# A hand-written order of operations in attention plus GELU MLP: k and q of batch 2 loaded ahead of its v, DMA transposes by heads, w_out released by the fourth of them

## The chip, the cores and the metric

The kernel runs on one core of one Trainium2 chip. The metric is device microseconds of one execution; lower is better. Input and output lie in HBM in float32.

## What is computed

The reference is an attention without softmax (squared ReLU of the scaled scores, divided by the sequence length), followed by a two-layer MLP with exact GELU:

```python
# q, k, v: 8 batches x 12 heads x 448 x 64;  w_in: 768 x 2048;  w_out: 2048 x 768
scores = (1 / sqrt(64)) * q @ k^T
attn   = maximum(scores, 0) ** 2 / 448
x      = (attn @ v), heads side by side -> 3584 x 768
h      = x @ w_in
out    = (0.5 * h * (1 + erf(h / sqrt(2)))) @ w_out        # 3584 x 768
```

## The kernel before

**Work and tiles.** The work is cut by batch (b = 0 to 7) and, inside a batch, into three groups of four heads (g = 0 to 2). Everything is computed in bfloat16; GpSimd's DMA queue casts on the way in. For each batch the steps are:

- *loads*: k (`add_k`, line 546), q (`add_q`, lines 467 and 469) and v (`add_v`, line 567), each as one DMA per group, issued by GpSimd (POOL). w_in comes in five pieces (`add_win`), w_out in three (`add_wout`, line 490): piece 0 is the right half of the columns (one DMA of 1536 KB), pieces 1 and 2 are the left half (two DMAs of 384 KB each).
- *transposes*: batches 0 and 1 are transposed on TensorE (`add_tk`, `add_tq`, lines 608 and 635) with copies by DVE or ACT. From batch 2 on, `add_T_dma` does it with DMA transposes issued by SP (line 668); the code calls one of them a `turn`. A batch has nine turns: for each group one of k, one of the even and one of the odd columns of q. The odd one of group g also reads the first columns of group g + 1, so it waits for that load of q too.
- *QK* (`add_steps`, line 742): seven steps per group, four 64x64 matmuls of 448 columns each; ReLU on ACT or DVE (lines 754, 756), square on DVE (line 763).
- *AV* (`add_av`, line 805): 28 matmuls per group; two copies to xT by DVE or ACT (lines 511, 513).
- *F1* (`add_f1`, line 857): x @ w_in, 16 products of six matmuls per batch, GELU on ACT (line 867).
- *F2*: the first 256 rows as four plain products of 16 matmuls (`add_plain`, line 1270); (0, 1) and (1, 1) need only piece 0 of w_out, (0, 0) and (1, 0) all three. Later rows go in groups of 256 with seven products of half the depth in place of eight (`add_group`, line 1175). Those need sums of w_out's quadrants, which DVE builds (`add_tsums`, line 1111). From batch 5 on F1 is done in the same way (line 1001).

**What sets the order.** The program builds a list of operations, each with the operations that it depends on and the buffers that it takes and frees. The string `ORDER` at the top gives, word by word, which operation is next on which engine: P for TensorE (PE), A for ACT, D for DVE, G for GpSimd, S for SP, Z for a filler matmul; the number is the operation's place in the list. `Scheduler.place` walks through this string. Every engine executes its own words strictly in that order, so an operation that waits holds up all later ones on its engine. Waits come from the dependencies; the planner's costs have no influence on an operation that stands in `ORDER`.

**Buffers that matter here.** k and q before their transposition lie in one buffer each (`nk`, `nq`) from batch 2 on, so the loads of batch b + 1 wait until the turns of batch b have read them. kT and qT have two buffers, so the turns of batch b wait for QK of batch b - 2. PSUM has three double banks for QK and AV and two single banks for everything else.

**The gates.** GpSimd's queue is in order. A tiny copy on GpSimd that reads a transposed tile therefore holds back every load behind it until that turn has landed:

```python
def add_gate(b, g):
    def fn(e):
        n = (16 * g + 1) * KC
        nc.gpsimd.tensor_copy(gate, get_T(b)[0][:, n : n + 16 * KC : KC])

    deps = [Tq[b, g, c][0] for c in range(NC)] + [Tk[b, g, 0][0]]
```

It waits for all turns of q and k of the group. `add_gate(2, 0)` stands ahead of the first w_out load, `add_gate(2, 1)` ahead of piece 2, `add_gate(2, 2)` ahead of the loads of batch 3.

Of the kernel before, what the change touches and what calls it, by code (L numbers as in the profile page):

```python
# [18 lines left out]
NK = S // KB  # L19
# [62 lines left out]


ORDER = """
G1435 G0 A10 Z512 Z512 Z512 D13 Z512 G1 A16 Z512 P11 P17 G7 G3 D12 D18 P14 P42 G4 G121 D15 P21 D22
A43 P39 G2 P19 D44 A40 D20 P36 P29 P33 P48 G5 D41 A37 P31 P51 A49 D30 P23 P54 D32 G118 D34 A52 G6
P25 D24 P93 D26 P27 P63 G117 A55 P69 A94 P133 A64 D38 D28 A70 P57 Z512 G122 G9 D35 D56 P45 P90 D50
D134 A58 G8 Z512 P66 A91 D46 D71 G125 D47 A67 P131 D59 P81 Z512 D65 D68 P84 P108 A82 D53 D132 A85
P129 A109 P72 D92 A73 G126 P60 G120 D130 D86 A61 P96 G124 A74 P135 P102 G119 A62 P143 G128 D83
G123 A97 P78 A103 P105 D95 G127 P75 D136 D98 A144 A79 G147 P141 P111 D76 D104 A106 A142 D80 D77  # L90
G148 P99 P156 A112 P137 A100 G149 P171 D101 P139 A157 A172 D107 P168 P87 G150 D113 D110 G151 P114
S231 A169 D88 D138 A89 P159 A115 D140 A160 P195 A116 P145 P162 A146 D196 P219 D161 P204 A163 P251
D205 P243 D164 G152 G153 A220 P165 D170 A252 D158 A244 D173 P174 P180 A175 A181 D166 P259 P249
S229 P189 D176 A250 S232 D167 D190 P213 S228 A214 G154 P177 A178 P222 A260 P192 P265 P247 A266
D206 G155 A193 P267 D223 P207 D197 A179 S230 A248 D194 P183 P210 A268 P263 P253 D221 A208 D182
D211 P198 D224 A184 A264 A254 S234 D209 P216 P186 D191 G237 A187 P261 D199 D188 D212 D200 D185
A262 P255 P245 A217 P201 D215 D218 P225 G238 A256 P257 P288 D202 S233 S235 D226 A246 G239 A227
D203 D289 A258 P285 P294 A295 P372 P362 D286 S236 A373 P291 G240 D292 P276 P300 A363 P378 P356
A277 A379 D296 P376 A357 G241 P352 P303 G242 D301 P312 A377 P306 A353 P350 D313 P380 A351 D390
A381 P368 P370 G269 A369 P358 G270 A371 A359 P364 A365 D314 P354 P282 A355 D302 D304 D307 A283  # L100
D293 G271 G272 P279 P318 P366 G273 P348 A367 A349 P360 D305 D278 A361 D284 P374 G274 P382 A375
D319 D290 A280 D308 G275 D391 P330 P309 D287 D281 S398 P297 A331 D392 D320 S399 P315 P384 A298
D393 S401 A310 D396 A383 D417 P387 D394 A385 D419 A299 D311 A316 D395 P324 D317 P321 D418 A325
D397 P333 A388 P327 P421 D420 D322 S400 A328 P423 D323 A334 D326 S386 D422 P339 S402 P336 P342
D424 P425 D329 G407 G408 S403 A343 D335 P427 G409 A426 D337 S389 P429 A340 S404 D428 D344 P431
S405 D338 D341 P440 D332 P437 P345 D430 A438 D441 G410 P443 G411 P446 D432 P433 S406 A346 G412
D347 A444 P509 A447 D434 P511 D439 S435 D448 A510 S436 D442 P449 P452 P455 S541 D562 A512 P513
D445 A453 P515 D454 A450 A514 S542 P517 D456 G413 G414 D451 G415 P464 D457 S543 P461 P458 G416
A465 D462 A518 P467 P470 A516 P519 A459 P521 D471 A520 D472 P523 D466 A468 D460 A522 D560 P479
P476 P473 D469 A524 P525 D463 A477 P527 D480 A474 S544 D478 A526 P529 D475 A528 D481 P488 P485  # L110
P482 A489 D486 S545 A530 P494 P491 G550 P531 G551 D487 D483 G552 S546 P533 D495 A532 A484 P535
S547 D496 D561 A492 D490 A534 P503 P500 P497 D493 A536 P537 P564 D498 A538 D504 P539 A501 S548
D499 G553 A565 D505 G554 P600 D502 P603 G555 P506 S549 A601 D604 A540 P606 P609 P566 D563 A507
# [282 lines left out]
def kernel(  # L396
# [9 lines left out]
    nc = tc.nc  # L406
# [88 lines left out]
    def get_T(b):  # L495
        if b not in qkT:
            qkT[b] = (
                tpool.tile([128, SLOTS * KC], BF16, tag="qT", name="qT"),
                tpool.tile([128, G, NK * 128], BF16, tag="kT", name="kT"),
            )  # L500
        return qkT[b]
# [13 lines left out]
    def e_copy(n, psum=4):  # L515
# [4 lines left out]
    sch = Scheduler({"w": 3, "a": NA, "f": 2, "osb": 3, "s1": 1, "s2": 1, "s3": 1, "s4": 1,  # L520
                     "p": 1})
    pool_q, pe_q = [], []
# [8 lines left out]
    Tq, Tk = {}, {}  # L531
# [55 lines left out]
    def add_wout(i):  # L587
        c, rows = WOUTS[i]

        def fn():  # L590
            for kf in rows:
                load_wout(kf, c)

        n = ND * sum(kf.stop - kf.start for kf in rows)
        ld_wout[i] = dma(fn, n * 128 * 4, issues=len(rows))
# [64 lines left out]
    def add_T_dma(b, after):  # L660


        after = [list(x) for x in after]

        def turn(dst, src, deps):
            return sch.add(
                (("SP", T_STEP, T_TIME),),
                lambda e: nc.sync.dma_start_transpose(dst(), src()),  # L668
                deps + old_T(b) + after.pop(0), mode="X",
            )  # L670

        def slots_of(n, o, k):
            return lambda: get_T(b)[0].rearrange("p (s t) -> p s t", t=KC)[
                :, 2 * n + o : 2 * (n + k) + o - 1 : 2
            ]

        def q_src(n, o, k):
            return lambda: nq[b][:, 128 * n + D * o : 128 * (n + k) + D * o]

        def k_dst(g):  # L680
            return lambda: get_T(b)[1][:, g].rearrange("p (i t) -> p i t", t=128)

        def k_src(g):
            return lambda: nk[b][:, 2 * g : 2 * g + 2].rearrange("p e f -> p (e f)")

        n0, odd = 0, None
        for g in range(G):
            op = turn(k_dst(g), k_src(g), list(ld_k[b, g]))
            for i in range(NK):
                Tk[b, g, i] = (op, op)  # L690
            lands = list(dict.fromkeys(ld_q[b, g, c] for c in range(NC)))
            n = 8 * g + 9
            even = turn(slots_of(8 * g, 1, 8), q_src(8 * g, 1, 8), lands)
            prior = odd or even
            beyond = [ld_q[b, g + 1, c] for c in range(NC)] if g < G - 1 else []
            beyond = list(dict.fromkeys(beyond))
            odd = turn(slots_of(n0, 0, n - n0), q_src(n0, 0, n - n0), lands + beyond)
            n0 = n
            for c, o in enumerate((even, odd, prior, odd)):
                Tq[b, g, c] = (o, o)  # L700

    gate = const.tile([128, 16], BF16, tag="gate", name="gate")

    def add_gate(b, g):


        def fn(e):
            n = (16 * g + 1) * KC
            nc.gpsimd.tensor_copy(gate, get_T(b)[0][:, n : n + 16 * KC : KC])  # L709

        deps = [Tq[b, g, c][0] for c in range(NC)] + [Tk[b, g, 0][0]]
        pool_q.append(sch.add((("POOL", 0.2, 0.3),), fn, deps))

    xT, hT = {}, {}
    readers = {}
# [684 lines left out]
        add_load(2, g, g + 1)  # L1400
    add_steps(steps(1), ATT1_BIAS, True)
    add_T_dma(2, [[]] * 9)
    add_gate(2, 0)
    add_wout(0)
    add_wout(1)
    add_gate(2, 1)
    add_wout(2)
    add_gate(2, 2)
    for m in range(0, HALF_M, 2):
        add_f1(0, m, 1, bias=F1B_BIAS)  # L1410
# [135 lines left out]
```

## Time and profile before

| | |
|---|---|
| median of 3 runs | 378.59 us (377.18 to 379.72) |
| profiled execution | 377.22 us |
| its span | 375.4 us, granted TensorE clock 0.995 |
| TensorE busy | 360.1 us, 96% of the span |
| VectorE (DVE), ScalarE (ACT), GpSimd (POOL) busy | 285.4, 198.7, 64.7 us |
| chain that ended last | TensorE 83%, DMA 6%, ACT 4%, DVE 3% |
| DMA | 47.27 MB, mean 126 GB/s; 202 GB/s in the busiest early slices |

The profile is of one execution. A line of the timeline gives start and length in us, the engine, the line of the kernel, what was done and how often; in square brackets stands how long the engine had been idle before it and what released it. DMA lines give the issuing queue, the size and the time from issue to landing. PE is TensorE's matmul stream, SPq the DMA queue of SP, POOLq that of GpSimd.

### The profile page before, as it was taken

The numbers are of one execution on the slowest core, as the hardware profiler recorded it, in microseconds if no ns is written. First come the engines' busy times: TensorE is split into PE (matmuls) and PEld (weight loads), VectorE is DVE, ScalarE is ACT, GpSimd is POOL, SyncE is SP. The second block draws the span as 40 slices with busy tenths as digits, with TensorE's granted clock in tenths as the row PEclk, the third lists the DMA queues.
The fourth block names the chain that finished last, engine by engine and source line by source line (L and its number), as shares of the span: only waits on it lengthen the run. The fifth ranks groups of instructions, "written<-read, shape, count | busy, mean of one in ns | idle before, by whom it ended". The sixth has DMA issues, their size and how long they took to land.

```text
span 375.4 us, 8364 instructions
## 1 busy us (share of the span) xinstructions
PE 360.1 (96%) x3517; PEld 219.3 (58%) x3517; DVE 285.4 (76%) x473; ACT 198.7 (53%) x319; POOL 64.7 (17%) x103
## 2 busy tenths in 40 slices
PE   7989998599999999999999999999999999999995
PEld 3666554245554445554455544456985897688663
DVE  2989875168888898989498996998868558755872
ACT  3988755145555663856876567764540263045200
POOL 8575404320231233012220000000000000000000
PEclk9999999899999999999999999999999999999999
DMA  9999999999999999999996980002002300310222
GB/s 169 202 201 205 202 181 167 182 201 178 156 200 196 160 204 159 202 188 184 182 158 103 201 166 3 0 2 84 2 2 84 86 3 15 99 57 0 86 84 84
DMA packets 87812, 47.27 MB, mean 126 GB/s; under 512 B 53856, under 2 KB 84320, under 8 KB 87776
## 3 DMA queue, kind: packets, MB, share of 16 engines
q0 software_dynamic: 31376, 22.45, 41.8%
q1 hardware_dynamic: 55760, 23.79, 32.7%
q8 instruction: 27, 0.44, 0.5%
q10 hardware_dynamic: 640, 0.51, 0.4%
q14 instruction: 9, 0.07, 0.1%
HBM read 45.61 MB, written 11.01 MB: 151 GB/s over the span
## 4 chain that ended last, share of the span: by engine, by line
PE 83%; DMA 6%; ACT 4%; DVE 3%; SPq 1%; issue 1%; POOL 0%; DVEq 0%; ACTq 0%; POOLq 0%
PE pso L1175 31%; PE psh L857 20%; PE pb L1001 13%; PE ps L742 8%; PE pav L805 7%; DMA wout_sb<-in_moe_w_out_dram 4%; ACT a_sq L754 4%; PE pso L1270 3%; DMA nq<-in_q_dram 2%; SPq L668 1%; DMA qT<-nq 1%; DVE a_sq L763 1%; DVE part L1038 1%; DVE a_sq L756 1%; PE tp L635 0%
## 5 line engine op out<-in xcount | busy, mean ns | idle before, releaser
L754 ACT ACTIVATE a_sq<-ps 128x896 bf16<-128x896 f32 (+1 forms) x120 | 105.0, 918 | 39.7 <-PE ps L742 39.5
L763 DVE TENSOR_TENSOR a_sq<-a_sq 128x896 bf16<-128x896 bf16 (+1 forms) x169 | 97.2, 616 | 14.0 <-ACT a_sq L754 13.6
L857 PE MATMUL psh<-xT,win_sb 128*128 128x448 bf16 (+1 forms) x516 | 96.6, 340 | 0.0
L857 PEld LDWEIGHTS <-win_sb 128*128 128x128 bf16 x516 | 48.0, 98 | 45.6 <-issue 9.7
L756 DVE TENSOR_SCALAR a_sq<-ps 128x896 bf16<-128x896 f32 x49 | 53.0, 1087 | 14.0 <-PE ps L742 13.9
L867 ACT ACTIVATE h_sb<-psh 128x448 bf16<-128x448 f32 x80 | 43.3, 549 | 27.6 <-PE psh L857 27.3
L1175 PEld LDWEIGHTS <-s_sb 128*128 128x128 bf16 x424 | 40.7, 98 | 26.7 <-issue 2.1
L1038 DVE TENSOR_TENSOR part<-pb,part 128x448 f32<-128x448 f32 x60 | 34.6, 620 | 21.5 <-PE pb L1001 21.5
L742 PE MATMUL ps<-qT,kT 64*64 64x448 bf16 (+1 forms) x756 | 48.0, 336 | 2.0 <-DMA qT<-nq 1.7
L1175 PEld LDWEIGHTS <-h_sb 128*128 128x128 bf16 x312 | 29.6, 98 | 21.9 <-issue 3.8
L805 PE MATMUL pav<-a_sq,v_sb 64*64 64x448 bf16 (+1 forms) x756 | 36.7, 329 | 1.7 <-issue 1.5
L1175 PE MATMUL pso<-wout_sb,s_sb 128*128 128x384 bf16 (+2 forms) x216 | 38.1, 320 | 0.1
L1175 PE MATMUL pso<-wout_sb,h_sb 128*128 128x384 bf16 x208 | 38.1, 326 | 0.0
L1175 PE MATMUL pso<-t_sb,s_sb 128*128 128x384 bf16 x208 | 38.1, 326 | 0.0
L742 PEld LDWEIGHTS <-kT 64*64 64x64 bf16 x756 | 18.3, 105 | 23.2 <-issue 17.4
L1047 ACT ACTIVATE h_sb<-part 128x448 bf16<-128x448 f32 x36 | 20.1, 578 | 20.2 <-DVE part L1038 19.9
L805 PEld LDWEIGHTS <-v_sb 64*64 64x64 bf16 x756 | 21.4, 107 | 13.4 <-issue 2.8
L1209 DVE TENSOR_TENSOR osb<-pso,p_sb 128x384 f32<-128x384 f32 x39 | 21.6, 554 | 10.0 <-PE pso L1175 7.4
L1001 PEld LDWEIGHTS <-win_sb 128*128 128x128 bf16 x288 | 27.6, 98 | 2.3 <-issue 0.4
L709 POOL COPY gate<-qT 128x16 bf16<-128x16 bf16 x15 | 5.7, 380 | 109.6 <-DMA qT<-nq 109.6
L1001 PEld LDWEIGHTS <-ws 128*128 128x128 bf16 x216 | 20.7, 98 | 0.0
L513 ACT CAST xT<-pav 128x448 bf16<-128x448 f32 (+1 forms) x33 | 16.0, 494 | 8.8 <-PE pav L805 5.6
(60 smaller groups left out, 295.4 us busy)
## 6 DMA issues: line engine op xcount, KB each, us to landing
nk<-in_k_dram POOLq DMA_DIRECT2D x23, 224.0 KB, 6.0
nq<-in_q_dram POOLq DMA_DIRECT2D x21, 224.0 KB, 6.8
out_dram<-osb SPq DMA_DIRECT2D x20, 192.0 KB, 3.8
v_sb<-in_v_dram POOLq DMA_DIRECT2D x5, 672.0 KB, 11.0
v_sb<-in_v_dram POOLq DMA_DIRECT2D x9, 224.0 KB, 9.0
out_dram<-osb SPq DMA_DIRECT2D x6, 336.0 KB, 2.9
win_sb<-in_moe_w_in_dram POOLq DMA_DIRECT2D x8, 192.0 KB, 9.1
wout_sb<-in_moe_w_out_dram POOLq DMA_DIRECT2D x1, 1536.0 KB, 14.4
```

Of the source, the lines that this page charges most:

```text
L742: nc.tensor.matmul(ps[64 * j : 64 * j + 64, e, x * w : x * w + w], kT[r, g, i * 128 + 64 * j : i * 128 + 64 * j + 64], moving, start=True, ...
L754: A.activation(ar, ps, AF.Relu, scale=c_att)
L756: V.tensor_scalar(ar, ps, c_att, 0.0, op0=mybir.AluOpType.mult, op1=mybir.AluOpType.max,)
L763: V.tensor_mul(box["a2"][:, :, :used], ar, ar)
L805: nc.tensor.matmul(pav[0][o2 : o2 + 64, e, :w], vt[b][r, 2 * g + e, bass.ts(i, D)], box["a2"][r, y, o : o + w], start=(i == 0), stop=(i == ...
L857: nc.tensor.matmul(ph[:, x * n : x * n + n], win_sb[:, kd, bass.ts(m + x, 128)], xT[b][:, kd, c], start=(kd == 0), stop=(kd == KD - 1),)
L867: A.activation(h_ring()[:, m : m + nm, o + c.start : o + c.stop], box[0][:, :S].rearrange("p (x n) -> p x n", x=nm), AF.Gelu,)
L1001: nc.tensor.matmul(bank[name][:, y, z * HS : z * HS + HS], w[:, k, bass.ts(mm, 128)], right()[:, k], start=first and k == 0 and z == 0, st ...
L1038: V.tensor_add(get(to), ps(name), get(other))
L1047: A.activation(h_ring()[:, m : m + 2, o + half[c].start : o + half[c].stop], src().rearrange("p (x n) -> p x n", x=2), AF.Gelu,)
L1175: nc.tensor.matmul(box[bank][:, n0:n1], left()[:, kf], right()[:, kf, n0:n1], start=bool(need) and kf == 0, stop=kf == K2 - 1, skip_group_ ...
L1209: V.tensor_add(out()[:, n0:n1], box[bank][:, n0:n1], other()[:, n0:n1])
```

## The change

One line of the program's list is exchanged, one small function is added for it, and `ORDER` is new up to about the ninth F1 product of batch 2:

```diff
+    def add_kgate(b, g):
+
+        def fn(e):
+            nc.gpsimd.tensor_copy(gate, get_T(b)[1][:, g, :: NK * 8])
+
+        pool_q.append(sch.add((("POOL", 0.2, 0.3),), fn, [Tk[b, g, 0][0]]))
...
     add_T_dma(2, [[]] * 9)
-    add_gate(2, 0)
+    add_kgate(2, 1)
     add_wout(0)
```

`add_kgate(2, 1)` waits for one turn alone, that of k of group 1. Lines behind it in the file move by six (709 becomes 708 for the old gate, 1270 becomes 1276, and so on).

`ORDER` has 26 changed lines of 79; a few of them:

```diff
-G1435 G0 A10 Z512 Z512 Z512 D13 Z512 G1 A16 Z512 P11 P17 G7 G3 D12 D18 P14 P42 G4 G121 D15 P21 D22
+D13 G0 A10 Z512 G1 Z512 G7 G1435 P11 P14 A16 D12 P17 D15 A18 P33 P19 P21 D20 A34 A22 P39 G3 P42
...
-A262 P255 P245 A217 P201 D215 D218 P225 G238 A256 P257 P288 D202 S233 S235 D226 A246 G239 A227
+P263 G238 D194 D191 P201 A264 D221 A256 S234 A202 P225 D226 P288 A203 P282 D227 P257 D289 A258
...
```

Read by queue, that is:

```
SP, turns of batch 2 (group: k, q even, q odd)
  before: k1 qe0 qe1 k0 qo0 k2 qo1 qe2 qo2
  after:  k0 qe0 qo0 k1 qe1 qo1 k2 qe2 qo2

GpSimd, from the loads of batch 2
  before: k0 q0 v0 k1 q1 v1 k2 q2 v2 gate(2,0) w_out0 w_out1 gate(2,1) w_out2 gate(2,2) loads of batch 3
  after:  k0 q0 v0 k1 q1 k2 q2 kgate(2,1) w_out0 v1 w_out1 v2 w_out2 gate(2,1) gate(2,2) loads of batch 3
  and the identity matrix (line 1330) made after the first three loads, not ahead of them

TensorE, from the last AV of batch 1 to the first QK of batch 3 (the number of operations)
  before: F1, 3 QK, 2 F1, 3 QK, 4 F1, 3 QK, F1, plain(0,1), 5 F1, 3 QK, 4 F1, plain(1,1), 2 QK, AV,
          QK, plain(0,0), plain(1,0), QK, AV, 2 QK, 2 products, 3 QK, 4 products, QK of batch 3
  after:  2 QK, F1, 3 F1, 3 QK, 4 F1, 3 QK, 2 F1, 3 QK, 3 F1, plain(0,1), 2 F1, 2 QK, AV,
          2 QK, 2 F1, plain(0,0), plain(1,1), 3 QK, product, plain(1,0), QK, QK of batch 3, AV, ...
```

The first F1 named is the last one of batch 0 in both, the others are of batch 1. Ahead of that AV the same operations stand on TensorE in another order, with two of the eight filler matmuls at the start and six further on (before: five and three). A few copies and ReLUs change between ACT and DVE (DVE 470 operations before and 469 after, ACT 317 and 318). No matmul, load or store is added or taken away.

More of the change, by code (lines that the diff above doesn't have):

```diff
@@ L84 @@
 ORDER = """
-G1435 G0 A10 Z512 Z512 Z512 D13 Z512 G1 A16 Z512 P11 P17 G7 G3 D12 D18 P14 P42 G4 G121 D15 P21 D22
[L86 to L95, printed above, removed]
@@ L96 @@
-D211 P198 D224 A184 A264 A254 S234 D209 P216 P186 D191 G237 A187 P261 D199 D188 D212 D200 D185
-A262 P255 P245 A217 P201 D215 D218 P225 G238 A256 P257 P288 D202 S233 S235 D226 A246 G239 A227
[L98 to L107, printed above, removed]
@@ L108 @@
-D445 A453 P515 D454 A450 A514 S542 P517 D456 G413 G414 D451 G415 P464 D457 S543 P461 P458 G416
-A465 D462 A518 P467 P470 A516 P519 A459 P521 D471 A520 D472 P523 D466 A468 D460 A522 D560 P479
-P476 P473 D469 A524 P525 D463 A477 P527 D480 A474 S544 D478 A526 P529 D475 A528 D481 P488 P485
+D13 G0 A10 Z512 G1 Z512 G7 G1435 P11 P14 A16 D12 P17 D15 A18 P33 P19 P21 D20 A34 A22 P39 G3 P42
+A43 Z512 P48 D40 D44 G4 P29 P36 D35 D30 P23 A49 P54 D24 A37 P51 G121 P25 D26 Z512 A52 A55 D41 P63
+P66 A67 P27 P90 D64 D50 G2 P31 P69 D28 G5 D32 A91 P57 Z512 D38 D53 Z512 Z512 G118 A58 D59 D65 P102
@@ new lines @@
+A103 D68 P93 A70 G6 P133 A94 P45 D46 D56 G117 G122 D134 P84 A47 G9 P129 P108 G8 D95 P60 A85 D61
+A109 P131 A62 P96 D71 P75 A97 D130 D132 P72 D73 Z512 P78 A76 P135 A74 A79 G125 P156 P143 G126 A157
+D86 P105 P111 G120 G124 D98 D136 A144 P165 A166 D92 D110 D77 D112 A106 D104 P141 D113 P81 P99 G119
+G128 D107 P139 D100 A82 D80 P162 A142 A101 P114 P174 D83 G123 D115 G127 A163 P137 G147 D116 A175
+P87 G148 A88 P159 D140 G149 P168 D138 A169 D89 D176 P145 S228 P243 G150 P210 A146 P183 D160 D167
+A244 P216 D161 P251 A184 A252 D217 P189 A211 P171 G151 S229 S230 D158 D170 S231 D185 P249 A172
@@ new lines @@
+P259 D164 D173 P198 A190 P180 A250 P177 A181 D199 P219 A260 G153 P186 P253 D212 D182 D218 S232
+A178 A220 D179 P247 D187 D200 A254 P207 P222 P195 A248 D223 P265 A208 D209 P261 A196 G154 A266
+D188 P204 S233 P192 P213 P245 D205 D224 A262 A214 D206 A246 D215 A193 G237 P267 D197 P255 A268
+P263 G238 D194 D191 P201 A264 D221 A256 S234 A202 P225 D226 P288 A203 P282 D227 P257 D289 A258
+P374 D283 P348 A375 P354 D290 P291 A349 D292 P300 P276 P366 D277 A355 G152 A367 D293 P364 A365
+A301 P358 P370 A359 P285 G239 P294 P279 S235 P350 D286 A371 A280 P372 G155 S236 P303 A295 P306
@@ new lines @@
+P312 A351 A373 G241 P356 P376 D281 G240 A357 P360 G242 A307 A377 G269 A361 P380 G270 D313 D308
+D302 D287 A381 D278 D284 A304 P362 D390 D314 P352 P342 D391 S398 D296 S399 A353 P318 D343 D344
+A319 P297 A298 P309 D392 G271 G272 P333 A363 D393 D394 D320 S401 P368 A369 P378 A379 D417 D299
+P384 D395 P382 A385 P330 A310 A334 P327 S400 P315 D418 G273 P421 A316 A328 D311 D305 A422 D383
+P387 A331 D397 P336 D317 P443 D396 P321 D419 D329 S386 D335 A337 P324 A388 P423 D322 P425 A444
+A325 D326 A323 D420 G274 D424 A426 P437 P449 D338 P339 D340 S402 G275 G407 D332 P427 G408 P429
@@ L111 @@
+P455 S403 A438 D428 A450 D341 G409 A456 D430 P440 D441 P345 P470 D560 P467 D562 D471 P431 D445
+A346 A347 D432 P433 A468 P446 D434 A447 D451 P452 P461 P513 A514 D453 P523 P521 D439 G410 A524
+P517 A522 G411 P515 G412 A518 A516 P511 D457 P509 D448 D454 D462 S389 S404 A512 D442 S405 A510
+P464 S406 A465 S435 P476 S436 P458 P479 S541 D477 G413 P473 G414 P519 P525 D472 G415 G416 A459
+A460 D466 D469 A520 S542 S543 D463 P527 D480 A474 S544 D478 A526 P529 D475 A528 D481 P488 P485
 P482 A489 D486 S545 A530 P494 P491 G550 P531 G551 D487 D483 G552 S546 P533 D495 A532 A484 P535
```

## The prediction

> **What bounds the kernel now.** I read the page first: the shares, the slices, the chain that ended last; then the PE timeline around its idle stretches, the waits of the queues, and windows of 2 us with the DMA columns.
>
> ```profile
> span 375.4 us, 8364 instructions
> PE 360.1 (96%) x3517; PEld 219.3 (58%) x3517; DVE 285.4 (76%) x473; ACT 198.7 (53%) x319; POOL 64.7 (17%) x103
> ...
> PE   7989998599999999999999999999999999999995
> ...
> DMA  9999999999999999999996980002002300310222
> ```
>
> TensorE is busy for 96% of the span, so only its 15 us without work and its slow stretches can be won. The slices (9.4 us each) put the losses into the first slices and into the eighth (the 5, 66 to 75 us). The DMA engines stand at 9 up to slice 22: in this part every transfer queues behind others. The PE timeline shows the two idle stretches and their releasers (start, length, engine, line, count, idle before):
>
> ```profile
> 54.82 1.31 PE L857 MATMUL psh<-xT,win_sb 128*128 128x448 bf16 x6
> 57.81 0.76 PE L742 MATMUL ps<-qT,kT 64*64 64x448 bf16 x12 [1.68 <-DMA qT<-nq]
> ...
> 66.91 1.31 PE L857 MATMUL psh<-xT,win_sb 128*128 128x448 bf16 x6
> 72.68 4.21 PE L1270 MATMUL pso<-wout_sb,h_sb 128*128 128x384 bf16 x16 [4.46 <-DMA wout_sb<-in_moe_w_out_dram]
> ...
> 87.73 2.76 PE L1270 MATMUL pso<-wout_sb,h_sb 128*128 128x384 bf16 x16
> ```
>
> The first QK of batch 2 waits 1.68 us for a turn (a DMA transpose) of q, the first plain product 4.46 us for w_out. That product then takes 4.21 us; the same sixteen matmuls take 2.76 at 87.73. The windows say why: the clock stood at 0.55 and 0.59.
>
> ```profile
> 68.00:70.00 2.00, 0.21 (x2) 0.00 (x0) 0.00 (x0) 0.54 (x1) 0.00 (x0) 1.00 1.27 192
> 70.00:72.00 2.00, 0.00 (x0) 0.00 (x0) 0.00 (x0) 0.00 (x0) 0.21 (x1) 1.00 1.32 199
> 72.00:74.00 2.00, 1.32 (x5) 0.65 (x6) 0.00 (x0) 0.00 (x0) 1.65 (x3) 0.55 1.32 203
> 74.00:76.00 2.00, 2.00 (x9) 1.02 (x8) 1.26 (x2) 0.00 (x0) 1.89 (x3) 0.59 1.31 205
> ```
>
> (Columns: window, length, busy PE, PEld, DVE, ACT, POOL, clock, DMA share, GB/s.) All engines stand still while the DMA engines run full. The chain names what holds them:
>
> ```profile
> 54.27 3.40 DMA qT<-nq
> 57.81 0.21 POOL gate L709
> 58.02 0.24 issue
> 58.26 14.37 DMA wout_sb<-in_moe_w_out_dram
> 72.68 4.21 PE pso L1270 x16
> ```
>
> The fifth turn lands at 57.7, the gate copy on GpSimd follows, w_out is issued at 58.26 and its first part lands 14.4 us later. From 76.7 to 248 us PE never idles, so whatever reaches PE in the front goes through to the end, as long as nothing later comes due too early.
>
> **The change, part by part.** From about the ninth product of F1 of batch 2 (PE at 124.96 us) on, the instructions of every engine stand in the same order in both kernels. So the question is when PE reaches that point.
>
> *k and q ahead of v, turns by heads.* In before, the copies of batch 2 land one behind another, about 1.15 us apart: k of group 0 at 43.0 (issue 34.21 + 8.8), k of group 1 at 46.4, the last q at 51.6 (42.32 + 9.3), the last v at 52.7 (43.26 + 9.4). SP's first turn wants k of group 1, so it starts at 46.51. In the changed kernel it wants k of group 0: SP starts at 43.0. A turn alone lands 3.2 to 3.4 us after its issue, and SP issues one every 1.3 us; but beside queued copies it crawls:
>
> ```profile
> kT<-nk SPq DMA_TRANSPOSE x1, 3.2
> ...
> qT<-nq SPq DMA_TRANSPOSE x1, 7.2
> ...
> qT<-nq SPq DMA_TRANSPOSE x1, 11.6
> ...
> kT<-nk SPq DMA_TRANSPOSE x1, 9.3
> ```
>
> (Four single issues, us to landing: at 52.9 with the copies drained, at 58.4 and 59.8 beside w_out, at 81.6 beside k and q of batch 3.) So the early turns gain little until the copies drain. One v fewer stands before the last q (1.3 us), and the identity matrix moved behind three DMA issues on GpSimd starts all loads some 0.3 us sooner: the copies drain at about 50.1 instead of 52.7. In before the first three turns land 0.7, 1.5 and 2.3 us after the drain; the same gives 50.8, 51.6 and 52.4, and group 0 is complete. QK of batch 2 is wanted at 54.7 (below): the 1.68 us go.
>
> *w_out after the fourth turn.* The fourth (k of group 1) is issued when SP is free, at 50.4, and lands 3.2 us later, 53.6. Landing to w_out's issue took 0.6 us (57.67 to 58.26): issue at 54.2, 4.0 us earlier. With 14.4 us its first part lands at 68.6. Bounds: 12.5 us (1.57 MB at the 203 GB/s of the full windows, plus the 4 to 5 us that a copy of 224 KB takes when the queue is short) and 18.1 us (the longest w_out issue): 66.7 to 72.3. In the single software queue two v copies (1.15 us each) now stand among the w_out parts, so its last part lands at 80.4 - 4.0 + 2.3 = 78.7.
>
> [...]
>
> *The new order on PE.* Ahead of the first plain product stand five more F1 (6 matmuls, 1.14 us each) and two more QK (0.2 us): 6.1 us of cover moved forward from behind it. From the end of the last AV of batch 1 (54.7): 13 F1 = 14.8 us and 11 QK in four bunches (0.50 for two, 0.69 for three from the chain's x8 and x12) = 2.6: PE arrives at 72.2 without idling. w_out is there at 68.6 (72.3 by the upper bound). So the 4.46 us go, and with them the slow clock, 4.04 us to the next product instead of 2.6: 1.45. Together 1.68 + 4.46 + 1.45 = 7.6 us. If the cover were gone, 4.46 would come back less the 4.0.
>
> *What is late next.* PE then runs on to the first QK of batch 3, which the new order places before the second AV of batch 2. From 72.2: four plain (10.4), four F1 (4.6), eight QK (2.2 with the changes of tile form), one AV (1.3), one product of group 1 (1.3): 92.0; the first QK of batch 3 stood at 108.5 before. It needs the last turn of group 0 of batch 3, which landed at 90.11 + 5.8 = 95.9. k and q of batch 3 queue behind w_out, whose end moves by 1.7 us: 94.2. With PE 0.3 us earlier (next part), 91.7, it waits 2.5 us; behind it in PE's queue stand the AV and all that follows, and DVE's copies of that AV wait as well. Bounds: 0 (the turns land early) and 5.5 (one more turn beside copies, 3.2 us more). The gates of groups 1 and 2 now follow the last w_out issue on GpSimd; they release k of batch 3 only when the last q turn lands, 71.3 before, some 72.5 now, and copies still queue until 78.7, which hides this.
>
> *The front up to 53 us.* PE's work there is the same. DVE and ACT are busy without a gap from 10 to 20 us, so order shifts little; the first q of group 1 lands 0.3 us sooner where PE waits 1.03 us. I take 0.3 us gained, between 1.5 lost and 2.0 gained (its own gaps sum to 3.2). The DVE sees one operation fewer (469 against 470) and is at most 95% busy in 90 to 100 us; no price.
>
> *Sum:* 7.6 + 0.3 - 2.5 = 5.4 gained; I take off 0.2 for DVE running late after the new stall: 5.2. The profiled execution took 377.22 us (span 375.4): 372.0. It lies 1.4 under the median of the runs shown (378.59; 377.18 to 379.72), so as a median **373.4 us**. About 1% is what a measurement of this kernel tells from no change.
>
> **The rivals.** (1) *The new stall does not come:* turns of batch 3 land by 92. For it: the DMA windows 50 to 52 (99 GB/s) and 58 to 62 (155, 127) hold some 2 us of unused transfer that earlier turns and w_out could fill. Then 7.6 - 0.2: 371.2. (2) *The stall grows and the clock falls with it:* a wait of 4 to 5 us and 1.5 us of half clock as after 72.7. Gain 7.9 - 4.5 - 1.5 = 1.9: 376.7. For it: the turns beside copies took 7 to 11 us. [...] (3) *Slower:* the third turn beside w_out starves until the copies end. Then the last q turn of batch 2 lands at 79 instead of 72.5, gate and k of batch 3 follow at 79.8, k lands 5.5 us later (as 96.61 to 102.1) at 85.3, and the last turn of group 0, 14.4 us behind it as in before, at 99.7. PE waits 7.6 us plus 1.5 of clock, 9.1 against 7.9 won: 379.8; it is a loss from 98.5 us on, and 383 if k of group 1 starves too. Against it: the two turns beside w_out landed 5.7 us apart, so a third lands by 73 if it starts 4 us sooner. (4) *The early release does nothing* since bytes rule: w_out lands at 72.6 as before. The new order still hides it, but batch 3 comes at 98: as (2) or (3).
>
> **How the numbers follow.** Forecast 0.55 (371 to 375.5), (1) 0.13, (2) with (4) 0.20, (3) 0.12. Faster by over 1% means under 374.8: 0.49 of the forecast and all of (1), 0.62; slower needs 382.4, the far half of (3) and accidents of the new front, 0.12; the rest 0.26. The range 370.2 to 379.6 reaches from (1) to (3).
>
> **What would show it.** Right: QK of batch 2 starts at 54 to 55 with no idle; w_out issued near 54, its first part landed by 70; the plain product at full clock; one PE idle of about 2 us on a turn of q at 92 to 95. Wrong: the gate copy after 56, a plain product still waiting, idle above 4 us at the first QK of batch 3, or new PE gaps before 50 us.

## The result and the profile after

The changed kernel takes 376.08 us (374.81 to 378.09) against 378.03 us (375.26 to 379.72) for the kernel before: a ratio of 0.9959, 95% interval 0.9940 to 0.9977. That is a gain of 1.6 us (0.9 to 2.3), where 5.2 had been forecast; 376.08 is near the 376.7 of rival (2). The two profiled executions lie closer together than the medians (376.74 against 377.22, spans 375.0 and 375.4; the one 0.7 above its median, the other 0.8 below), so what follows accounts for the 0.5 us between them; the rest of the gain is not in this pair. The granted clock may hold a part of it: of 29 executions of the kernel before that were measured beside the later experiments, 26 had a mean clock of 0.988 to 0.993 and only three the 0.995 of the profiled one, while 13 of the changed kernel's 17 had the 0.990 or 0.991 of its profile. So the profiled execution of the kernel before lost less to the half clock than most.

The page of the changed kernel, its span, shares and slices:

```profile
span 375.0 us, 8360 instructions
PE 361.1 (96%) x3517; PEld 219.8 (59%) x3517; DVE 284.2 (76%) x472; ACT 200.5 (53%) x320; POOL 63.5 (17%) x103
...
PE   8999999997599999999999999999999999999995
...
DMA  9999999999999999999998970002002300310222
```

TensorE's weak slices have moved: the eighth (66 to 75 us) is full now, the tenth and eleventh (84 to 103 us) are the 7 and the 5. The PE timeline says by what (start, length, engine, line, count, idle before and its releaser):

```profile
54.02 0.55 PE L748 MATMUL ps<-qT,kT 64*64 64x448 bf16 x8
...
68.25 3.58 PE L863 MATMUL psh<-xT,win_sb 128*128 128x448 bf16 x18
71.66 2.76 PE L1276 MATMUL pso<-wout_sb,h_sb 128*128 128x384 bf16 x16
...
91.46 0.38 PE L748 MATMUL ps<-qT,kT 64*64 64x448 bf16 x4
97.61 0.59 PE L748 MATMUL ps<-qT,kT 64*64 64x448 bf16 x4 [5.77 <-DMA qT<-nq]
```

Both old stalls are gone: QK of batch 2 starts at 54.02 with no idle before it, the first plain product at 71.66, at once and at full clock (2.76 us, not 4.21). In their place stands one stall of 5.77 us at the first QK of batch 3. The windows of 2 us around it show its second price:

```profile
92.00:94.00 2.00, 0.00 (x0) 0.00 (x0) 0.00 (x0) 1.18 (x2) 0.00 (x0) 1.00 1.35 158
94.00:96.00 2.00, 0.00 (x0) 0.00 (x0) 0.00 (x0) 0.00 (x0) 0.00 (x0) 0.73 1.28 147
96.00:98.00 2.00, 0.39 (x8) 0.26 (x12) 0.00 (x0) 0.00 (x0) 0.21 (x1) 0.50 1.15 227
98.00:100.00 2.00, 2.00 (x28) 1.20 (x24) 0.00 (x0) 0.92 (x1) 1.43 (x2) 0.50 1.22 225
100.00:102.00 2.00, 2.00 (x20) 0.74 (x12) 0.62 (x1) 0.77 (x1) 0.00 (x0) 0.57 1.12 70
```

(Columns as before: the last three are granted clock, DMA share, GB/s.) The clock falls at 94.9 and comes back at 101.7, 6.8 us at half speed. The AV at 97.95 takes 2.61 us to the next start instead of 1.32, and with the operations around it that is 2.0 us lost after the stall itself. The chain of waits names the way there:

```profile
49.67 4.71 DMA kT<-nk
54.38 0.05 issue
54.44 0.20 POOL gate L716
...
92.61 4.87 DMA qT<-nq
97.47 0.14 issue
97.61 0.59 PE ps L748 x4
```

The fourth turn lands at 54.38 and w_out is issued at 54.67, 3.6 us sooner than before. But the last part of w_out lands at 82.38, where it was 80.39 before (two v copies now stand among its parts, 2.3 us by the prediction's 1.15 us each), and the turn that QK of batch 3 wants lands at 97.47, where it was 95.92.

The balance of the two profiles at the ninth F1 product of batch 2, from which the orders agree: 7.59 us of old stalls and slow clock gone, 0.7 won in the front (the last AV of batch 1 starts at 52.70, before 53.39), 5.77 and 2.0 lost. That is 0.5 us, and the product starts at 124.51 instead of 124.96.

### The profile page after: what moved, and what is told of

The parts are those of the page before. It is cut to its first block, busy times and chain, and to the rows that moved or that the text cites. A ratio compares the mean times of both kernels' runs of the same rounds, so it can differ in the third digit from the quotient of the medians.

```text
span 375.0 us, 8360 instructions
## 1 busy us (share of the span) xinstructions
PE 361.1 (96%) x3517; PEld 219.8 (59%) x3517; DVE 284.2 (76%) x472; ACT 200.5 (53%) x320; POOL 63.5 (17%) x103
## 4 chain that ended last, share of the span: by engine, by line
PE 73%; DMA 18%; SPq 3%; DVE 2%; issue 1%; POOL 1%; ACT 0%; DVEq 0%; POOLq 0%; ACTq 0%
PE pso L1181 31%; PE psh L863 16%; PE pb L1007 13%; PE ps L748 7%; DMA nq<-in_q_dram 6%; PE pav L811 6%; DMA wout_sb<-in_moe_w_out_dram 4%; SPq L668 3%; DMA win_sb<-in_moe_w_in_dram 3%; DMA nk<-in_k_dram 2%; DMA qT<-nq 1%; DMA kT<-nk 1%; DVE a_sq L769 1%; PE pso L1276 1%; DVE part L1044 1%
## 5 line engine op out<-in xcount | busy, mean ns | idle before, releaser
L760 ACT ACTIVATE a_sq<-ps 128x896 bf16<-128x896 f32 x120 | 105.7, 918 | 38.4 <-PE ps L748 37.9
L762 DVE TENSOR_SCALAR a_sq<-ps 128x896 bf16<-128x896 f32 (+1 forms) x49 | 52.5, 1077 | 16.4 <-PE ps L748 16.2
L811 PE MATMUL pav<-a_sq,v_sb 64*64 64x448 bf16 (+1 forms) x756 | 38.0, 338 | 1.0 <-issue 0.8
L511 DVE CAST xT<-pav 128x448 bf16<-128x448 f32 (+1 forms) x22 | 11.7, 545 | 14.0 <-PE pav L811 13.8
L708 POOL COPY gate<-qT 128x16 bf16<-128x16 bf16 x14 | 4.2, 301 | 101.4 <-DMA qT<-nq 101.4
## 6 DMA issues: line engine op xcount, KB each, us to landing
wout_sb<-in_moe_w_out_dram POOLq DMA_DIRECT2D x1, 1536.0 KB, 16.1
```

What stands on the lines that cost most here:

```text
L760: A.activation(ar, ps, AF.Relu, scale=c_att)
L762: V.tensor_scalar(ar, ps, c_att, 0.0, op0=mybir.AluOpType.mult, op1=mybir.AluOpType.max,)
L811: nc.tensor.matmul(pav[0][o2 : o2 + 64, e, :w], vt[b][r, 2 * g + e, bass.ts(i, D)], box["a2"][r, y, o : o + w], start=(i == 0), stop=(i == ...
```

## The experiments

Theory A: the gain was lost at one place, the first QK of batch 3, to the late landing of its turn and the half clock behind it; and the turn is late because turns and copies run side by side for longer, which costs both. The rivals: the transfers would only hand the wait on; or the earlier release of w_out is good in itself and something else lost the time.

**QK of batch 3 later.** Only the order on TensorE (and of two ReLUs on ScalarE to match) is changed:

```diff
-P336 P443 P321 P324 P423 P425 P437 P449 P339 P427 P429 P455 P440 P345 P470 P467 P431
+P336 P321 P324 P423 P425 P339 P427 P429 P443 P437 P449 P345 P455 P440 P431 P470 P467
```

> The changed kernel with one edit in the order of TensorE: the first three QK of batch 3 (443, 437, 449) stand behind the fifth product of group 1 (429) instead of one and three products ahead of it, so TensorE has an AV, four products and a few QK (some 7.6 us of work) to do before it asks for the turn of q that lands at 97.5. Theory A (the change lost its gain at this one wait: 5.77 us of idling, then 6.83 us at half clock, which cost some 2.0 us more): both go, 7.8 us less than the changed kernel, 368.3 us, the first AV behind them at 92 takes 1.3 us to the next instead of 2.6, and the first F1 that both kernels share in order starts near 117. Theory B (the transfers set the end and only hand the wait on): TensorE waits again within the next 15 us, for QK of group 1 or for batch 4, and the gain over the changed kernel stays under 4 us, 372 or more.

Measured: 371.18 us (369.60 to 374.38), ratio to the kernel before 0.9844 (0.9812 to 0.9877). The PE timeline of this run:

```profile
97.42 1.47 PE L1178 MATMUL pso<-t_sb,s_sb 128*128 128x384 bf16 x8
98.81 0.76 PE L745 MATMUL ps<-qT,kT 64*64 64x448 bf16 x12
100.21 1.52 PE L808 MATMUL pav<-a_sq,v_sb 64*64 64x448 bf16 x28 [0.64 <-ACT a_sq L757]
```

The turn lands at 97.63, no sooner than in the changed kernel, and nobody waits for it: QK starts at 98.81 behind products. The ninth F1 product starts at 118.01, 6.5 us sooner, and the span is 6.1 shorter; by the medians it is 4.9. Of the 7.8 expected, 1.04 went to two new short stalls (0.64 at the AV, 0.40 behind it). The time is 2.9 us above theory A's 368.3, but the wait and the half clock (mean clock 1.00 in the profiled execution) are gone and no wait of more than 0.64 us comes in their place, so theory B's handed-on wait did not come: the place is shown.

**Only the clock.** Two runs put zero matmuls into the stall, 18 of 512 columns each, to hold the clock.

```diff
-P443
+Z512 (18 times) P443        # first run: 18 operations, each takes a bank
+Z9216 P443                  # second run: one operation of 18 matmuls in one bank
```

> The changed kernel with 18 matmuls of zeros (64x512, 0.21 us each at full clock, 3.8 us together) ahead of the first QK of batch 3; they compute nothing that is used and lie in the time in which TensorE waits for the turn of q. They can start only when the eviction of the plain product before them has freed a bank, some 1.5 us after 91.8. Theory A (2.0 us of the loss is the half clock that follows the long idle): the idle stretch is split into pieces under 2 us, the clock stays at 1.00 from 96 to 103 us, and the end comes 2.0 us sooner: 374.1 us. Theory B (what follows the wait is slow for another reason, an engine that feeds TensorE or a wait for w_out's tail): the clock column rises but the time stays within 0.5 us of the changed kernel's 376.1, or is some tenths longer because the fillers delay the QK.

> The filler run again, with the 18 matmuls of zeros (64x512) in one bank and one operation, so that none waits for a release by the one before: in the first such run each took 0.60 us from start to start instead of 0.21, they ran on beyond the landing of the turn, and the clock fell at about 95 although TensorE had stood still for only 1.39 us. They start near 93.5 and end at 97.4. Theory A (TensorE kept busy keeps its clock, and the half clock after the wait costs 2.0 us): the clock stays at 1.00 and the time is 374.1 us. Theory B (such matmuls of zeros on 64 rows do not count as work for the clock): it falls at about 95 again, the later fillers take 0.43 us, QK of batch 3 starts about 1 us after its turn has landed, and the time is 377 to 378 us.

Measured: 383.96 us (382.56 to 385.62) for the first, ratio 1.0180 (1.0153 to 1.0207); 376.16 (374.09 to 378.44) for the second, ratio 0.9957 (0.9924 to 0.9990). The fillers of the first run and then of the second in the PE timelines:

```profile
93.62 10.80 PE L1513 MATMUL fill<-zero 64*64 64x512 bf16 x18 [1.39 <-ACT osb L511]
103.95 0.85 PE L746 MATMUL ps<-qT,kT 64*64 64x448 bf16 x4
```

```profile
92.33 4.08 PE L1513 MATMUL fill<-zero 64*64 64x512 bf16 x18 [1.39 <-ACT osb L511]
96.91 0.38 PE L746 MATMUL ps<-qT,kT 64*64 64x448 bf16 x4 [0.51 <-DMA qT<-nq]
```

As 18 operations they took 0.60 us each, the clock fell among them (0.68 in the window from 94 to 96, 0.50 from 96 to 98), and they outlasted the landing of the turn by 7 us: the first run shows only that such fillers are worse than the stall. As one operation they took 4.08 us, the profiled execution kept its clock at 1.00, and took 374.09 us as theory A had it. But the clock held in only 7 of the 12 executions (mean clock 0.997 or more, median 374.6 us) and fell in the other 5 (0.990 or less, median 378.0); 1.39 and 0.51 us of idling remain around them, but why it fell in just these is not shown. So, by the executions that kept their clock, the half clock is worth about 1.5 us against the changed kernel, not quite the 2.0 forecast, and the filler is no remedy: it costs more when it fails.

**What makes the turn land.** Two edits of the queues, each alone.

```diff
-S398 S399 S401 S400 ...        # SP: turn of k of group 1 ahead of q of group 0
+S398 S399 S400 S401 ...
```

> The changed kernel with two neighbours of SP's queue exchanged in batch 3: the third turn of group 0 (q, 400) is issued ahead of the first turn of group 1 (k, 401). In the changed kernel 401 is issued at 89.17 and 400 at 92.61, and 400 lands at 97.47, 4.9 us after its issue. Theory A (the wait of TensorE is the landing of that turn and nothing else): 400 is issued near 89.2 and lands near 94.1, TensorE idles some 2.4 us instead of 5.77, short enough that the clock stays at 1.00, so 3.4 + 2.0 = 5.4 us come back: 370.7 us. Theory B (a turn lands when the copies beside it have drained, whenever it was issued: the last copy, v of batch 3, landed at 95.1): it lands at 96 or later, the idle is 4 us or more and the clock still falls: 374 to 375 us.

Measured: 374.69 us (374.20 to 375.74), ratio 0.9932 (0.9911 to 0.9952). The turn in the DMA view at 88.0, and the stall on the PE timeline:

```profile
qT<-nq SPq DMA_TRANSPOSE x1, 7.1
```

```profile
95.31 0.59 PE L745 MATMUL ps<-qT,kT 64*64 64x448 bf16 x4 [4.18 <-DMA qT<-nq]
```

The turn is issued at 88.05 instead of 92.61, 4.6 us sooner, and lands at 95.17, 7.1 us after its issue instead of 4.9. The copy of v lands at 93.57 here, and the turns of group 0 at 93.45, 94.30 and 95.17. In the changed kernel v lands at 95.09, and the turns at 95.05, 95.82, 96.59 and 97.47. So theory B of this run was right in the main: the turns land when the copies have drained, 0.8 us apart. Of the 2.3 us by which this one lands sooner, 1.5 came with the copies, which end sooner in this execution, and 0.8 is the one step that the exchange saves; that is also why it landed ahead of theory B's 96. TensorE still idles 4.18 us and loses the clock (0.58 in the window from 94 to 96).

```diff
-G275 G407 G408 G409 ...        # GpSimd: v of batch 3, then gate and loads of batch 4
+G407 G408 G409 G275 ...
```

> The changed kernel with the load of v of batch 3 (672 KB) moved on GpSimd's queue behind the gate of group 0 of batch 3 and the first two loads of batch 4, so no copy of v stands beside the turns of group 0. Theory A (copies beside turns cost both of them): the copies of batch 3 end near 91.5 instead of 95.1, the last turn of group 0 lands 2 to 3.5 us sooner, at 94 to 95.5, and TensorE idles 2.3 to 3.5 us instead of 5.77, at the border of the clock's fall: 370.7 to 374. Theory B (the turn waits for SP's queue, whose issues take 3 to 4 us each, and not for the copies): the landing stays at 97 and the time at 376; and if v, which then lands some 10 us later, is late for the first AV of batch 3 (121.6 us), it is longer than 376.

Measured: 372.95 us (370.92 to 375.36), ratio 0.9892 (0.9860 to 0.9924). The single issue of that turn, in the DMA view at 90.3, and the stalls on the PE timeline:

```profile
qT<-nq SPq DMA_TRANSPOSE x1, 3.2
```

```profile
93.62 0.38 PE L745 MATMUL ps<-qT,kT 64*64 64x448 bf16 x4 [1.69 <-DMA qT<-nq]
104.47 0.57 PE L745 MATMUL ps<-qT,kT 64*64 64x448 bf16 x8 [1.02 <-ACT xT L510]
```

With 672 KB of copies out of the way the last copy lands at 90.19, the four turns at 90.72 to 93.49, and the stall is 1.69 us at full clock (1.00 in the windows from 92 to 96). That is theory A's expectation (94 us or later) and a little better; a later wait of 1.02 us takes some of it back. Both runs together show what set the landing here: while copies still ran, their end, and hardly the time of issue (4.6 us sooner brought 0.8). Once they had drained it was the issue: the fourth turn was issued at 90.33, behind the last copy, and landed 3.2 us later, like a turn alone (3.2 to 3.4 us in the kernel before).

**The release of w_out.** The fourth turn against the ninth:

```diff
-    add_kgate(2, 1)
+    add_gate(2, 2)
```

> The changed kernel with w_out released by the ninth turn of batch 2 instead of the fourth, so that no turn of batch 2 runs beside w_out. Theory A (turns and copies side by side cost both, so an early release wins little): the turns land about 3.2 us after their issue, 1.3 us apart, the ninth near 63 instead of 73.8; w_out is issued there, 8 to 9 us later than in the changed kernel, but its first part lands only 3 to 4 us later, at 74 to 75, and the last of batch 3's group 0 at 98 to 99, 1 us later than 97.5. TensorE waits 2 to 3 us at the first plain product and 3 to 4 us at QK of batch 3: 377 us, within 1.5 us of the changed kernel. Theory B (a queue is a queue: what is issued 8.5 us later lands 8.5 us later): w_out's first part at 79, the turn at 106, 384 us or more.

Measured: 378.88 us (377.69 to 380.69), ratio 1.0039 (1.0013 to 1.0065). Its last three turns of batch 2 and last two parts of w_out in the DMA view, and then the same issues of the changed kernel:

```profile
kT<-nk SPq DMA_TRANSPOSE x1, 3.3
...
qT<-nq SPq DMA_TRANSPOSE x1, 5.0
...
qT<-nq SPq DMA_TRANSPOSE x1, 4.5
...
wout_sb<-in_moe_w_out_dram POOLq DMA_DIRECT2D x2, 384.0 KB, 16.6
```

```profile
kT<-nk SPq DMA_TRANSPOSE x1, 7.2
...
qT<-nq SPq DMA_TRANSPOSE x1, 12.5
...
qT<-nq SPq DMA_TRANSPOSE x1, 15.4
...
wout_sb<-in_moe_w_out_dram POOLq DMA_DIRECT2D x2, 384.0 KB, 21.9
```

Alone, the three turns land within 5 us; beside w_out within 7 to 15. And w_out with the two v copies in its queue takes 21.95 us from first issue to last landing without turns (62.87 to 84.82) and 27.7 with them (54.67 to 82.38): 5.8 us for the three turns issued behind w_out, with the last 1 to 2 us of the two issued just ahead of it. Each figure is of one profiled execution; in the eight that have the changed queues of batch 2 the same stretch took 25.9 to 27.7 us, so the price lies between 3.9 and 5.8. An issue 8.2 us later thus ended only 2.4 us later, and the turn of batch 3 landed at 99.42, 1.95 us later. That is near theory A's row (98 to 99), not theory B's 106. Yet the early release is worth having, since without it the first part comes at 74.86 and the plain product waits 2.79 us. The two stalls of this run:

```profile
74.90 4.33 PE L1273 MATMUL pso<-wout_sb,h_sb 128*128 128x384 bf16 x16 [2.79 <-DMA wout_sb<-in_moe_w_out_dram]
99.55 0.59 PE L745 MATMUL ps<-qT,kT 64*64 64x448 bf16 x4 [3.27 <-DMA qT<-nq]
```

I had expected 377; the clock fell at both stalls (0.67 in the window from 74 to 76, 0.64 from 98 to 100), and the whole is 2.8 us worse than the changed kernel.

**The two halves of the change apart.** The orders of the computing engines of one kernel with the queues of SP and GpSimd (and the release of w_out) of the other:

```diff
 # run 1: P, A and D words of the changed kernel
-    add_kgate(2, 1)
+    add_gate(2, 0)              # and the S and G words of the kernel before
 # run 2: P, A and D words of the kernel before
 #        add_kgate(2, 1) and the S and G words of the changed kernel
 # run 3: as run 1, with QK of batch 3 later as in the first experiment
```

> The orders of TensorE, ScalarE and VectorE of the changed kernel, with the queues of SP and GpSimd of the kernel before: loads and turns in the old order, w_out released by the copy that waits for the whole of group 0 of batch 2. Theory A (the queues' part of the change removes the front's wait but delays batch 3; TensorE's order does the rest): QK of batch 2 is reached at 54.0 as in the changed kernel and waits until 57.7 as before, 3.7 us; the first plain product comes 3.7 us later, near 75.3, and does not wait, since w_out lands at 72.6 as before; QK of batch 3 is reached near 95.5 and its turn lands at 95.9 as before, so the 5.77 us and their half clock go. Balance against the changed kernel: 3.7 lost, 5.4 + 2.0 won, 372.4 us; 374 if the 3.7 us make the clock fall. Theory B (earlier loads, turns and w_out are worth what they were meant for): without them the time is above the changed kernel's 376.1, by up to the 3.7 us.

> The reverse: the queues of SP and GpSimd and the release of the changed kernel, with the orders of TensorE, ScalarE and VectorE of the kernel before (the identity matrix first on GpSimd, as before). Theory A (the earlier release moves w_out's first part by 1.85 us only, and the cover for it is TensorE's order): QK of batch 2 is reached near 56.1 and does not wait; the first plain product is reached near 66.5 and waits until w_out lands at 70.8, 4.3 us, with the half clock behind it as before; QK of batch 3 stands at 108 and never waits. The gain over the kernel before is 1.9 us: 376.1 us. Theory B (the release as forecast: w_out at 68.6): the wait is 2.1 us, the clock holds, and 5.5 us are won: 372.5 us.

> The late QK of batch 3 with the queues of SP and GpSimd and the release of w_out of the kernel before: the fourth corner of the comparison, which tells what the queues' part of the change is worth when no wait at batch 3 takes it back. Theory A (it is worth the wait at QK of batch 2 alone): 2.4 us of idling at QK of batch 2 as in the run with the old queues, w_out and batch 3 covered, so 2.4 us more than 371.2: 373.6, and the 0.95 us of that run's wait at batch 3 gone, within 0.7 us of its 373.5. Theory B (the earlier release of w_out is worth something beyond that): 375 us or more, with a wait at the first plain product. Theory C (the queues' part is worth nothing even then): 371.2 us.

| order of the computing engines | old queues | new queues |
|---|---|---|
| before | 378.03 | 377.18, ratio 0.9981 (0.9954 to 1.0007) |
| changed | 373.52, ratio 0.9882 (0.9844 to 0.9921) | 376.08, ratio 0.9959 (0.9940 to 0.9977) |
| changed, QK of batch 3 later | 374.64, ratio 0.9909 (0.9888 to 0.9930) | 371.18, ratio 0.9844 (0.9812 to 0.9877) |

The medians come from different sets of runs; each ratio is to the kernel before as it ran in the same set, so the ratios are the safer comparison.

Stalls in run 1, then in run 2:

```profile
56.93 0.57 PE L745 MATMUL ps<-qT,kT 64*64 64x448 bf16 x8 [2.38 <-DMA qT<-nq]
95.38 0.38 PE L745 MATMUL ps<-qT,kT 64*64 64x448 bf16 x4 [0.95 <-DMA qT<-nq]
```

```profile
69.98 5.30 PE L1274 MATMUL pso<-wout_sb,h_sb 128*128 128x384 bf16 x16 [4.47 <-DMA wout_sb<-in_moe_w_out_dram]
```

The new order of the computing engines does the work: with the old queues it gains more than the whole change does (373.52 us, inside theory A's 372.4 to 374, with a wait of 2.38 us where 3.7 was expected). The new queues alone are not told from nothing: TensorE reaches the plain product 2.7 us sooner and waits 4.47 us for w_out again, with the half clock behind it. Theory A gave 376.1 there and the run took 1.1 more; the half clock lasted 6.8 us in its profile, from 69.0 to 75.8, and 3.4 us in that of the kernel before. Only together with the later QK do the new queues pay, 3.5 us by the medians (371.18 against 374.64) and 2.5 by the ratios: without them TensorE idles 2.88 us at QK of batch 2, more than the 2.4 expected, and the clock falls with it; so run 3 took 1.0 us more than theory A's 373.6, though nothing waits at the plain product as theory B had it. The windows of that third run:

```profile
54.00:56.00 2.00, 0.08 (x4) 0.00 (x0) 1.16 (x2) 0.00 (x0) 0.00 (x0) 1.00 1.04 204
56.00:58.00 2.00, 1.04 (x9) 0.35 (x10) 0.41 (x1) 0.00 (x0) 0.79 (x2) 0.62 0.88 166
58.00:60.00 2.00, 2.00 (x7) 0.78 (x6) 2.00 (x3) 0.00 (x0) 2.00 (x3) 0.53 0.76 138
```

**One step further.** The three late QK behind the next AV as well, to take away the 0.64 us:

```diff
-P429 P443 P437 P449 P345 P455 P440
+P429 P345 P443 P437 P449 P455 P440
```

> As the run with the late QK of batch 3, but the three QK (443, 437, 449) stand one operation later still, behind the second AV of batch 2's last group (345). In that run they took the three banks in PSUM just ahead of the AV, which waited 0.64 us until ScalarE had emptied one. Theory A (after the wait for the turn is gone, TensorE has only such small stalls left): the 0.64 us go and nothing comes in their place, 370.5 us. Theory B (ScalarE and VectorE are behind, and any order waits as long somewhere in the next 10 us): no change, 371.2 us.

Measured: 372.64 us (372.16 to 374.13), ratio 0.9864 (0.9840 to 0.9888): not faster than the run that it was to improve (0.9844, 0.9812 to 0.9877; the intervals overlap). The AV now waits 0.59 us for VectorE in its midst, and the QK behind it 0.82, 0.42 and 0.43 us for banks that ScalarE empties. Theory B was right: here ScalarE and VectorE are the limit. The first experiment remains the version with the lowest median, ahead of both kernels.

## Why the prediction went wrong, point by point

- *The old stalls, 7.6 us:* right. QK of batch 2 starts at 54.02 (54.7 forecast), w_out is issued at 54.67 (54.2), PE reaches the plain product at 71.66 without idling (72.2), and the slow clock there is gone. There was little to spare: group 0 of batch 2 was to be complete at 52.4, and its last turn landed at 53.63, 0.4 us ahead of the QK that needs it.
- *w_out's first part at 68.6:* wrong by 2.2 us (70.78, inside the bounds of 66.7 to 72.3): the issue came 0.5 us later than forecast, and from issue to landing passed 16.1 us, not 14.4. It cost nothing, since the new order covered it; with the old order it would have (run 2).
- *The front, 0.3 us:* 0.7.
- *PE at QK of batch 3 at 91.7:* right, 91.84.
- *The last w_out part at 78.7, and with it the turn at 94.2:* this is the step that failed. The second half of it was right: from the last w_out part to the fourth turn of batch 3 pass 15.5 us before, 15.1 after, 14.6 to 16.0 in the runs that left the loads and turns of batch 3 in their order. The first half was not: 82.38 instead of 78.7. I moved w_out's end with its issue and added the two v copies; I had seen that a third turn would run beside w_out, and priced it for the turns, not for the copies. The turns beside w_out were slow indeed (7.2 to 15.4 us), but for what the turns cost the copies the sum had no price. The run with the ninth turn gives one: 21.95 us for w_out and the two v copies without turns, 27.7 with three beside them. The sum allowed 24.4 us (the kernel before's 22.1, which holds the price of its two turns, and 2.3 for v). So the sum put at nothing the 3.3 us that the turns cost the copies beyond the two turns of before; the rest of the miss is the issue at 54.67 instead of 54.2. Hence 97.47 and a stall of 5.77 us, just over the 5.5 that I had as its bound.
- *The clock:* a wait of 2.5 us was to leave it alone, so no term stood for it in the sum. That was not shown: the kernel before had stalls of 1.68 us (clock 1.00) and 4.46 us (0.55 in the window of the restart), none between. The wait became 5.77 and cost 2.0 us more, as rival (2) had it. Nor would 2.5 us have been sure to leave the clock alone: of the stalls in the other runs' profiles 2.38 us left it at 1.00 and 2.79 us did not.
- *Rival (3), the third turn starving until 79:* it landed at 73.79. *Rival (4), the early release does nothing:* for the first part half so (issued 3.6 us sooner, landed 1.85 sooner, 72.63 to 70.78), and for what comes behind w_out less than nothing.
- *Two slips that changed nothing:* 54.7 + 14.8 + 2.6 is 72.1, not 72.2, and the range ends at 379.6, 0.2 short of the 379.8 of rival (3).

The sum with the measured terms is 7.6 + 0.7 - 5.8 - 2.0 = 0.5, which is what the two profiles differ by.

## What to carry to other kernels

The transfer that was released earlier beside others did not end earlier by as much (w_out: issued 3.6 us sooner, its first part landed 1.85 us sooner, its last 2.0 us later); price what such a transfer runs beside, for both sides, and follow the queue's end to its next consumer. When a new order pulls an operation forward by many microseconds, ask when its input lands, not only whether the stalls before it go: here moving three QK back by seven microseconds of work was worth more than the whole change. Split a change by engines before judging it: the half that seemed to be its purpose, the new queues, could not be told from nothing alone, cost 2.6 us beside the new order (376.08 against 373.52), and paid only when QK of batch 3 stood later.

## What the hardware showed that I had not expected

- In batch 3 the DMA transposes landed when the copies beside them had drained, 0.8 us apart, almost whenever they were issued: in the changed kernel turns issued at 83.62, 84.94, 89.17 and 92.61 landed between 95.05 and 97.47, the last copy at 95.09; in the run with v later between 90.72 and 93.49, the last copy at 90.19. It is no general rule: with QK of batch 3 later the third of these turns landed 2.1 us behind the second, in the kernel before the first landed at 90.97, 2.7 us ahead of the last copy (93.63), and beside w_out turns landed at 62.21, 68.83 and 73.79 while w_out ran until 82.38.
- The clock fell sooner than I had assumed. Stalls of 1.68, 1.69 and 2.38 us left it at 1.00 in the profiled executions; stalls of 2.79 and 2.88 us did not (0.67 and 0.62 in the window of the restart). But the length of a stall did not decide alone: in the first run with fillers the clock fell (0.68 in the window from 94 to 96) though the stall ahead of them was only 1.39 us; why is not shown. Nor can 2.38 us be called safe: the profiled execution of that kernel had a mean clock of 0.999, but the other five had 0.994 or 0.995, and 0.995 is what the kernel before had in its profile, with one stretch at half speed. Once fallen, the clock stayed at half for 3.4 us in the kernel before (72.2 to 75.6) and in the third run above (56.5 to 59.9), and for 6.8 us in the changed kernel (94.9 to 101.7).
- Zero matmuls that each take their own bank took 0.60 us from start to start and did not hold the clock (mean 0.982 to 0.987 in the six executions); the same matmuls in one bank took 0.23 us each (4.08 us for 18) and held it in 7 of 12 executions (mean 0.997 or more).
